# Batch 0's transposes on TensorE, the sign as a bit, and two token groups in one pass over the weights

## The chip, the cores and the metric

The kernel runs on one core of a Trainium2 chip. The metric is the device time of one execution in microseconds (us). Its five engines (TensorE or PE, VectorE or DVE, ScalarE or ACT, GpSimd or POOL, SyncE or SP) each work through their own queue in order, and the 16 DMA engines move data beside them. The time before is the median of three runs.

## The reference

Causal attention with a decay, then a SwiGLU block, then a mixture of eight experts of which each token uses one:

```python
q, k, v: (4, 8, 576, 64)   f: (4, 8, 576)          # batch, head, position, dim
cum    = cumsum(log(clip(f, 1e-4, 1)))
scores = q @ k.T / 8 + cum[:, None] - cum[None, :]   # causal
x      = softmax(scores) @ v                          # -> (2304, 512)
h      = silu(x @ w_gate) * (x @ w_val)               # (512, 1536), float64 weights
y      = h @ w_out                                    # (1536, 512), float64
e      = argmax(y @ r_gate); p = softmax(y @ r_gate)[e]
out    = p * (relu(y @ w1[e]) @ w2[e])                # 8 experts, 512 x 1024 x 512
```

## The kernel before

**Three stages.** Attention goes over 16 pairs of heads, four pairs (`NP`) to a batch. A pair has four items: two heads, each with the first three blocks of queries (g=0) and the last two (g=1). `slot(i)` runs `part1` (scores, maximum, exponential) of item i, `part2` (the split of the probabilities into a high and a low 16-bit half, and their transposition) of item i-1, and `pv` (probabilities times v) of item i-2. The SwiGLU block goes over nine groups of 256 tokens, in six units each (j, 256 of the 1536 inner columns): `unit_g` and `unit_v` make 24 TensorE products each into the banks `g` and `v`, a Tanh on ScalarE (L526), two VectorE steps (L529, L536), a split, and `unit_o` one unit later adds 12 products (L556) to the two banks `y0` and `y1`; `fin0` copies these out when a group is complete. The experts are the third stage.

**Weights.** The three SwiGLU weights arrive as float64. `decode` makes a float32 tile of 128 x 512 from a fetch of 512 KB, looked at as pairs of 32-bit words `lo` and `hi`: ScalarE takes the absolute value of `hi` as a float (L878) and its sign (L879), VectorE shifts by three bits (L880) and joins the top bits of `lo` (L881), GpSimd multiplies by the sign (L884). There are 36 of these. `w_dec`, `w_split` and `wo_dec` are the tasks round them; `mark[j]` and `markw[j]` say which tasks unit j needs. Fetches land in `wgb`, `wvb` while those are free, and in the one buffer `raw`.

**Transposition by DMA.** `prep` scales q and k of a head, splits them into halves (L230, L234, L235) and has a DMA transpose them from `qks` to `qkt` (L237). `score` adds two products, (qh, kh) and (qh, kl side by side with ql), and a decay term and mask. `part2` casts a row of probabilities to 16 bits (L349, VectorE), subtracts for the low half (L352, L363, GpSimd) and has a DMA transpose the lot into `pt` (L366), which `pv` reads (L387). After the second head, `xn` is normalised (L400) and for batch 0 transposed by TensorE (L429) into `xr`, the input of the units, by L440 (ScalarE) and L441 (VectorE).

**Order.** Python code emits the slots, tasks and units in a fixed sequence, and a scheduler with a timeline of its own sets each engine's queue from it. First 18 slots (`first`, batch 0) with 43 tasks among them; then units 0 to 53, each preceded by the tasks it needs (`mark[u]`, six units) and by slots that `pace` hands out along the points `pts_`: none until unit 4, batch 1 until unit 10, and so on.

```python
pts_ = [(-1, first), (NJ - 2, first), (2 * NJ - 2, 8 * NP + 2), (4 * NJ - 1, 12 * NP + 2), (6 * NJ - 2, NSL)]
```

PSUM has eight banks: three for scores, one for `px`, and one each for `g`, `v`, `y0`, `y1`.

Of the kernel before, what the change touches and what calls it, by code (L numbers as in the profile page):

```python
# [27 lines left out]
def kernel(  # L28
# [37 lines left out]
    g_d = dram.tile([NT + 1, 1], F32, name="g_d")  # L66
# [19 lines left out]
    cnt = const.tile([128, NE], F32, name="cnt")  # L86
    sv = const.tile([128, 2, B], F32, name="sv")
# [9 lines left out]
    def consts():  # L97
# [32 lines left out]
        vec.memset(cnt, 0.0)  # L130

# [24 lines left out]
    qk_in = [ap_.tile([128, 2, NCH, D], F32, name=f"qk_in{i}") for i in range(NQK)]  # L156
# [16 lines left out]
    def load_heads(t, src, b, h):  # L173
        sp.dma_start(out=t[64:128, :, 0, :], in_=src[b, h:h + 2, 0:64, :].rearrange("h p d -> p h d"))
        for hh in range(2):
            sp.dma_start(
                out=t[:, hh, 1:NCH, :], in_=src[b, h + hh, 64:S, :].rearrange("(c p) d -> p c d", p=128)
            )

    def load_qk(P, a):  # L180
        if P < NPAIR:
            load_heads(qk_in[(2 * P + a) % NQK], (q, k)[a], P // NP, 2 * (P % NP))
# [32 lines left out]

    def prep(P, hh):
        sc, c = stt[P]
# [20 lines left out]
        heads[P, hh] = (qkt, c[1][:, hh, :])  # L238
# [129 lines left out]

    pxs = {}

    def pv(i):
# [9 lines left out]
        for m in range(nt):  # L381
            last = base + m
            pm, o = pt[m]
# [136 lines left out]

    def unit_g(u):
        g, j = divmod(u, KF // 2)
# [9 lines left out]
    def unit_v(u, t):  # L532
        g, j = divmod(u, KF // 2)
# [12 lines left out]
    def unit_o(u):  # L546
        g, j = divmod(u, KF // 2)
        hi, lo = hbuf.pop(u)
        if j == 0:
            yps[g] = [ps_y.tile([128, DM], F32, tag=f"y{i}", name="yp") for i in range(2)]  # L550
        for i in range(2):
            n_ = 0
            for fi in range(2):
                fk = 2 * j + fi
                for hx, wx in ((hi, 0), (hi, 1), (lo, 0)):
# [4 lines left out]
                        start=(j == 0 and n_ == 0),  # L560
                        stop=(j == KF // 2 - 1 and n_ == 5),
# [76 lines left out]
    def fin2(g):  # L638
# [96 lines left out]
        rows_out(g_d, g, gw)  # L735
# [37 lines left out]
    def start():  # L773
# [25 lines left out]
        act.dma_start(out=g_d[NT:NT + 1, :], in_=zr[:, 0:1])  # L799
# [71 lines left out]
    def decode(src, n):  # L871
        c = c_tile()
        raw = fetch(src, n, c.rearrange("p (a n) -> p a n", a=n))
        if raw is not None:
# [3 lines left out]
            act.activation(out=c, in_=hi.bitcast(F32), func=ACTF.Abs, scale=2.0 ** -112)  # L878
            act.activation(out=hi.bitcast(F32), in_=hi, func=ACTF.Sign)  # L879
# [4 lines left out]
            gp.tensor_tensor(out=c, in0=c, in1=hi.bitcast(F32), op=ALU.mult)  # L884
# [37 lines left out]
    NJ = KF // 2  # L922
# [179 lines left out]
    def unit(u, between=None):  # L1102
# [5 lines left out]
        if u > 0:  # L1108
            if u - 1 < NJ:
                upto(markw[u - 1])  # L1110
            unit_o(u - 1)
            g1, j1 = divmod(u - 1, NJ)
# [10 lines left out]
            if j1 == NJ - 1:  # L1123
                if g1 == 0:
# [23 lines left out]
    PRE0, PRE = 2, 43  # L1148
# [16 lines left out]
    pts_ = [(-1, first), (NJ - 2, first), (2 * NJ - 2, 8 * NP + 2), (4 * NJ - 1, 12 * NP + 2), (6 * NJ - 2, NSL)]  # L1165
# [7 lines left out]
    for u in range(NU + 1):  # L1173
        if u < NJ:
            upto(mark[u])
        if u < NU and u % NJ == 0:
            for b, _, _ in spans(min(u // NJ + 1, NG - 1)):
# [4 lines left out]
        if u < NU:  # L1182
            need = 4 * NP * ((G * (u // NJ + 1) - 1) // S + 1) + 2
        tgt = pace(u)
        slots(need)
        unit(u, lambda: slots(min(tgt, nslot[0] + 1)))
# [162 lines left out]

    def gate(s, t):  # L1350
# [129 lines left out]
```

## Time and profile before

| what | us |
|---|---|
| runs, median of 3 (lowest to highest) | 1014.65 (1012.99 to 1016.63) |
| the profiled execution | 1012.41 |
| its span | 1010.6 |
| busy: PE / DVE / ACT / POOL | 882.2 / 614.9 / 555.3 / 389.6 |

The profiled execution is one run with the hardware profiler; its time and its span, from the first instruction to the last, differ by 1.8 us. Rows of a timeline have start and duration in us; consecutive instructions overlap a little. In lists by line, the two numbers after the count are busy us in all and mean ns of one. An arrow in a wait list points at what released the wait. PEclk is the granted clock of TensorE as a share of 2.4 GHz.

### The profile page before, as it was taken

To read this page: it belongs to the slowest core of one execution; us is meant where nothing else is said; L and a number is where in the kernel's file an instruction comes from. 1 tells how busy PE (TensorE), PEld (TensorE's weight loads), DVE (VectorE), ACT (ScalarE), POOL (GpSimd) and SP (SyncE) were. 2 spreads that over 40 slices of the span, in tenths; PEclk is the share of its full clock that TensorE was granted. 3 is DMA by queue.
4 is the path that set the end of the run, shared out by engine and by line. 5 is a ranking of instruction groups with operands and counts; after the bars stand their busy time and mean duration, and the time that the engine had idled before them with its cause. 6 is when DMAs were issued, how large, how long until landed. Compare 5 with 4: busy or idle time off the path is not lost.

```text
span 1010.6 us, 19838 instructions
## 1 busy us (share of the span) xinstructions
PE 882.2 (87%) x7028; PEld 734.7 (73%) x7053; DVE 614.9 (61%) x1818; ACT 555.3 (55%) x1205; POOL 389.6 (39%) x467
## 2 busy tenths in 40 slices
PE   1545557998999989999999999898989999999995
PEld 0334336877777868888878888687869788889894
DVE  6999888487666746565644434334536675665540
ACT  5987988476677666665633322122425454555431
POOL 1468676464444425344442222222245632100101
PEclk9995657999999999999999999899989999999998
DMA  8897998347886787567545422112376887765420
GB/s 244 209 216 205 230 204 187 90 101 165 180 172 146 164 190 158 101 133 137 102 113 143 121 22 64 5 18 66 71 180 187 218 219 201 215 198 159 132 95 34
DMA packets 309481, 146.35 MB, mean 145 GB/s; under 512 B 273441, under 2 KB 285857, under 8 KB 309380
## 3 DMA queue, kind: packets, MB, share of 16 engines
q1 hardware_dynamic: 305088, 134.68, 56.2%
q0 software_dynamic: 4096, 10.24, 3.7%
q8 instruction: 56, 0.92, 0.4%
q14 instruction: 45, 0.37, 0.2%
q10 hardware_dynamic: 196, 0.14, 0.0%
HBM read 84.24 MB, written 10.31 MB: 94 GB/s over the span
## 4 chain that ended last, share of the span: by engine, by line
PE 46%; DMA 17%; issue 12%; DVE 6%; ACT 3%; SPq 2%; POOL 2%; POOLq 0%; DVEq 0%; ACTq 0%
PE yp L556 11%; PE g L503 10%; PE v L503 10%; DMA out_dram<-o,ix 5%; PE bank L1218 3%; DMA pt<-p 3%; PE px L387 2%; DMA pair<-yt 2%; PE bank L1261 2%; DMA pair<-words 2%; DMA wr<-in_moe_w_dram 1%; PE ps L262 1%; PE ps L263 1%; DVE wlo L978 1%; PE ps L265 1%
## 5 line engine op out<-in xcount | busy, mean ns | idle before, releaser
L352 POOL TENSOR_TENSOR p<-st,p 128x128 f16<-128x128 f32 (+3 forms) x128 | 110.1, 864 | 102.1 <-issue 62.7
L543 POOL TENSOR_TENSOR lo<-t,hi 128x512 fp32r<-128x512 f32 x54 | 70.1, 1299 | 149.3 <-ACT hi L542 121.6
L503 PE MATMUL g<-xr,wga 128*128 128x256 f16 x864 | 106.1, 277 | 0.3 <-DVE t L529 0.3
L503 PE MATMUL v<-xr,wva 128*128 128x256 f16 x864 | 106.2, 277 | 0.0
L327 ACT ACTIVATE st<-st,nb,c 128x64 f32<-128x64 f32 (+4 forms) x160 | 102.6, 643 | 0.9
L503 PEld LDWEIGHTS <-wga 128*128 128x128 f16 x864 | 82.6, 100 | 17.2 <-issue 6.6
L503 PEld LDWEIGHTS <-wva 128*128 128x128 f16 x864 | 84.8, 101 | 10.6 <-issue 0.3
L387 PE MATMUL px<-vs,pt 128*128 128x64 f16 x1280 | 56.3, 203 | 39.3 <-DMA pt<-p 28.8
L349 DVE CAST p<-st 128x64 f16<-128x64 f32 (+4 forms) x160 | 68.4, 442 | 31.6 <-ACT st L327 20.1
L317 DVE CUSTOM_DVE_ANT_0 st<-ps,zero 128x64 f32<-128x64 f32 (+3 forms) x160 | 55.8, 377 | 50.9 <-PE ps L270 48.8
L387 PEld LDWEIGHTS <-pt 128*128 128x128 f16 x1280 | 50.3, 105 | 49.3 <-DMA pt<-p 32.8
L363 POOL TENSOR_TENSOR p<-st,p 128x64 f16<-128x64 f32 (+1 forms) x128 | 54.1, 424 | 70.6 <-issue 36.4
L262 PE MATMUL ps<-qkt 128*128 128x64 f16 (+2 forms) x192 | 56.5, 312 | 21.1 <-DMA qkt<-qks 7.2
L526 ACT ACTIVATE t<-g,gscale 128x512 f32<-128x512 f32 (+3 forms) x72 | 39.4, 573 | 62.2 <-PE g L503 59.0
L1012 POOL DMA_INDIRECT out_dram<-o,ix x24 | 24.6, 1026 | 123.3 <-ACT o L1263 79.5
L542 ACT ACTIVATE hi<-t 128x512 fp32r<-128x512 f32 x54 | 33.8, 625 | 56.5 <-DVE t L536 56.5
L556 PE MATMUL yp<-wohi,hi 128*128 128x512 f32 x144 | 60.6, 421 | 0.0
L263 PE MATMUL ps<-qkt 128*128 128x64 f16 (+2 forms) x192 | 60.1, 315 | 0.0
L1223 ACT ACTIVATE h<-bank 128x320 fp32r<-128x320 f32 (+1 forms) x64 | 26.3, 422 | 60.1 <-PE bank L1218 59.8
L1225 DVE SCALAR_TENSOR_TENSOR h<-bank,h 128x64 fp32r<-128x64 f32 (+2 forms) x128 | 33.4, 305 | 40.4 <-ACT h L1223 40.4
L556 PE MATMUL yp<-wohi,lo 128*128 128x512 f32 x144 | 57.6, 402 | 0.0
L556 PE MATMUL yp<-wolo,hi 128*128 128x512 f32 x144 | 57.1, 397 | 0.0
(322 smaller groups left out, 2483.2 us busy)
## 6 DMA issues: line engine op xcount, KB each, us to landing
wr<-in_moe_w_dram SPq DMA_DIRECT2D x72, 512.0 KB, 5.1
vr<-in_v_dram SPq DMA_DIRECT2D x16, 288.0 KB, 4.5
qk_in<-in_q_dram SPq DMA_DIRECT2D x32, 128.0 KB, 2.5
qk_in<-in_k_dram SPq DMA_DIRECT2D x32, 128.0 KB, 2.6
v_in<-in_v_dram SPq DMA_DIRECT2D x32, 128.0 KB, 3.0
y_d<-ys SPq DMA_DIRECT2D x6, 512.0 KB, 3.5
wgb<-in_moe_w_gate_dram SPq DMA_DIRECT2D x5, 512.0 KB, 5.9
raw<-in_moe_w_val_dram SPq DMA_DIRECT2D x5, 512.0 KB, 4.2
```

The source lines that it names most:

```text
L262: pe.matmul(out=ps[:, o:o + n], lhsT=lq, rhs=qkt[:, 1, k0:k1], start=True, stop=False, skip_group_check=True)
L263: pe.matmul(out=ps[:, o:o + n], lhsT=lq, rhs=qkt[:, 2, k0:k1], start=False, stop=False, skip_group_check=True)
L317: vec.tensor_tensor_reduce(out=sts[m][:, k0 - 64:k1 - 64], in0=ps[:, o:o + n], in1=zero.to_broadcast([128, n]), scale=1.0, scalar=init, op ...
L327: act.activation(out=sts[m], in_=sts[m], func=ACTF.Exp, scale=c[:, 0:1], bias=nb[:, m:m + 1], accum_out=sm[:, m, hh:hh + 1],)
L349: vec.tensor_copy(out=flat[:, o + 64:o + 64 + n], in_=src)
L352: gp.tensor_tensor(out=flat[:, o1:o1 + n - 64], in0=src[:, 64:n], in1=flat[:, o + 128:o + 64 + n], op=ALU.subtract)
L363: gp.tensor_tensor(out=blk[:, :, 0:64], in0=pair, in1=blk[:, :, 64:128], op=ALU.subtract)
L387: pe.matmul(out=px[:, 128 * m + 64 * hh:128 * m + 64 * hh + 64], lhsT=pm[:, o + ph * last + c, :], rhs=vs[:, hh, c, vh, :], start=(c == 0 ...
L503: pe.matmul(out=ps[:, fi, :], lhsT=w16[:, kk, wi, 128 * fi:128 * fi + 128], rhs=xr[:, kk, x0:x0 + 2, xi, :], start=(n_ == 0), stop=(n_ == ...
L526: act.activation(out=t[:, :, c0:c1], in_=gps[:, :, c0:c1], func=ACTF.Tanh, scale=gscale[:, b, j:j + 1])
L543: last["lo"] = gp.tensor_tensor(out=lo, in0=t, in1=hi.bitcast(F32), op=ALU.subtract)
L556: pe.matmul(out=yps[g][i], lhsT=hx[:, fi, 128 * i:128 * i + 128], rhs=wo[fk][wx], start=(j == 0 and n_ == 0), stop=(j == KF // 2 - 1 and n ...
```

## The change

**Order of units.** Units no longer run group by group at the start: `order` is group 0's units 0 to 2, all six of group 1, group 0's units 3 to 5, and then the rest as before. So weights of unit j are used by two groups in one sweep. Group 0's sums of the first three units are copied from `y0`, `y1` to DRAM by `part_out` and read back in `fin0(0)`, which adds them to the sums of the last three. 27 tasks instead of 43 stand among the first 18 slots; the others come during units 0 to 4, and those from the 19th on are fetched no earlier than q of batch 1's first pair. `pts_` loses the point that held batch 1 back until unit 4.

**Sign as a bit.** `decode` copies `hi` with its sign (Copy in place of Abs), drops the Sign and the multiplication, and lets VectorE join the sign bit of `hi` (L1003).

**Batch 0 without DMA transposes.** `prep0` transposes q and k of a pair as float32 on TensorE (L250), two heads at once, and ScalarE and VectorE split them from PSUM (L256, L257, L263, L264); the heads are kept apart by masks in the scale `qm`, which makes three products of a score where two were. `turn_p` transposes the float32 probabilities on TensorE (L449, 4 blocks a bank, banks `g`, `v`, `y0`, `y1` in turn), ScalarE copies the high half (L453) and VectorE subtracts for the low one (L454). Batches 1 to 3 keep the DMA transposes.

**Gate weights.** They were written to DRAM and gathered for the overflow tile; now `gate_of` computes them anew from that tile's x.

```diff
+    ring4 = [(ps_g, "g"), (ps_g, "v"), (ps_y, "y0"), (ps_y, "y1")]
...
+    def prep0(P):
+        sc, c = stt[P]
+        qm = st_p.tile([128, 2], F32, tag="qm", bufs=2, name="qm")
+        vec.tensor_scalar(out=qm, in0=half, scalar1=sc[:, 0, 0:1], scalar2=None, op0=ALU.mult)
...
+            for x in range(NCH):
+                o = ps[:, 128 * x:128 * x + 128] if x < NCH - 1 else last_[:, 128 * a:128 * a + 128]
+                pe.transpose(out=o, in_=src[:, :, x, :], identity=ident)
...
+                        act.activation(out=two[h][:, 0, n0:n1], in_=p, func=ACTF.Copy, scale=qm[:, h:h + 1])
+                        vec.scalar_tensor_tensor(
+                            out=two[h][:, 1, n0:n1], in0=p, scalar=qm[:, h:h + 1], in1=two[h][:, 0, n0:n1],
+                            op0=ALU.mult, op1=ALU.subtract,
+                        )
...
+            heads[P, h] = ([(qh, kh), (ql, kh), (qh, kl)], c[1][:, h, :])
...
+    def turn_p(i):
...
+        for blks in BLKS[g]:
+            ps = quad()
+            for x, (m, c) in enumerate(blks):
+                src = st[:, 0:128] if m == 0 else sts[m - base][:, max(128 * c - 64, 0):max(128 * c + 64, 128)]
+                pe.transpose(out=ps[:, 128 * x:128 * x + 128], in_=src, identity=ident)
...
+            act.activation(out=h_, in_=ps[:, 0:128 * w], func=ACTF.Copy)
+            vec.tensor_tensor(out=l_, in0=ps[:, 0:128 * w], in1=h_, op=ALU.subtract)
...
+    CUT = 3
+    order = (
+        [(0, j) for j in range(CUT)] + [(1, j) for j in range(NJ)] + [(0, j) for j in range(CUT, NJ)]
+        + [(g, j) for g in range(2, NG) for j in range(NJ)]
+    )
...
+    def part_out():
+        r = [c_p.tile([128, DM], F32, tag="c", name="yc") for _ in range(2)]
+        act.activation(out=r[0], in_=yps[0][0], func=ACTF.Copy)
+        vec.tensor_copy(out=r[1], in_=yps[0][1])
+        for i in range(2):
+            sp.dma_start(out=y_d[r0_of(i):r0_of(i) + 128, :], in_=r[i])
...
+        if g == 0:
+            rows_out(y_d, g, ys, True)
+            for i in range(2):
+                vec.tensor_tensor(out=ys[:, i, :], in0=ys[:, i, :], in1=yps[g][i], op=ALU.add)
...
-            act.activation(out=c, in_=hi.bitcast(F32), func=ACTF.Abs, scale=2.0 ** -112)
-            act.activation(out=hi.bitcast(F32), in_=hi, func=ACTF.Sign)
+            act.activation(out=c, in_=hi.bitcast(F32), func=ACTF.Copy, scale=2.0 ** -112)
...
-            gp.tensor_tensor(out=c, in0=c, in1=hi.bitcast(F32), op=ALU.mult)
+            vec.scalar_tensor_tensor(
+                out=ci, in0=hi, scalar=-2 ** 31, in1=ci, op0=ALU.bitwise_and, op1=ALU.bitwise_or
+            )
...
+            if done[0] < 18:
+                tasks[done[0]]()
+            else:
+                with tc.issue_after(qload[4, 1].ins):
+                    tasks[done[0]]()
...
-    PRE0, PRE = 2, 43
+    PRE0, PRE = 2, 27
...
-    pts_ = [(-1, first), (NJ - 2, first), (2 * NJ - 2, 8 * NP + 2), (4 * NJ - 1, 12 * NP + 2), (6 * NJ - 2, NSL)]
+    pts_ = [(-1, first), (2 * NJ - 2, 8 * NP + 2), (4 * NJ - 1, 12 * NP + 2), (6 * NJ - 2, NSL)]
...
+        if u < 2 * NJ:
+            upto(27 + (len(tasks) - 27) * (u + 1) // 5)
...
+    def gate_of(xt, ps, pool, dst):
+        p = ps("t")[:, 0:NE]
+        prods = [(x, kk) for kk in range(KD) for x in xt]
+        for n_, (x, kk) in enumerate(prods):
+            pe.matmul(
+                out=p, lhsT=x[:, kk, 0:128].bitcast(F32), rhs=rg[:, kk, 0:NE], start=(n_ == 0),
+                stop=(n_ == len(prods) - 1), skip_group_check=True,
+            )
```

VectorE's queue, in batch 0's slots, where weights are decoded between the items. Before:

```order
L880 TENSOR_SCALAR wo<-wo 128x512
L349 CAST p_1_108<-st 128x64
L349 CAST p_1_108<-st 128x192
L349 CAST p_1_108<-st 128x320
L881 SCALAR_TENSOR_TENSOR wo<-wvb,wo 128x512
L880 TENSOR_SCALAR wo<-wo 128x512
L881 SCALAR_TENSOR_TENSOR wo<-wgb,wo 128x512
L349 CAST p_2_109<-st 128x448
L349 CAST p_3_110<-st 128x576
L880 TENSOR_SCALAR wo<-wo 128x512
```

The place that answers to it after the change (L999 and L1000 are the shift and the join that were L880 and L881):

```order
L1003 SCALAR_TENSOR_TENSOR wo<-wgb,wo 128x512
L454 TENSOR_TENSOR p_1_108<-g,pt 128x512
L1003 SCALAR_TENSOR_TENSOR wo<-wvb,wo 128x512
L257 SCALAR_TENSOR_TENSOR qk_506<-ps,qm,qk_506 128x128
L1000 SCALAR_TENSOR_TENSOR wo<-raw,wo 128x512
L999 TENSOR_SCALAR wo<-wo 128x512
L935 TENSOR_SCALAR sw<-tot 128x1
L938 COPY sw<-tot 128x1
L454 TENSOR_TENSOR p_2_109<-v,pt 128x512
L454 TENSOR_TENSOR p_2_109<-yp,pt 128x128
```

The casts of the probabilities are gone from the row, and sign joins (L1003) and subtractions from PSUM (L454, L257) stand between the decoding steps.

SyncE's queue in the same part. Before:

```order
L861 DMA wvb<-in_moe_w_val_dram 128x4x256
L366 DMA_TRANSPOSE pt<-p_0_107 128x9x128
L174 DMA v_in_106<-in_v_dram 64x2x64
L176 DMA v_in_106<-in_v_dram 128x4x64 x2
L187 DMA v_in_106<-in_v_dram 64x2x64
L237 DMA_TRANSPOSE qkt<-qks 128x15x128
L366 DMA_TRANSPOSE pt<-p_1_108 128x9x128
L237 DMA_TRANSPOSE qkt<-qks 128x15x128
L366 DMA_TRANSPOSE pt<-p_2_109 128x7x128
L366 DMA_TRANSPOSE pt<-p_3_110 128x9x128
```

After (L981 is the weight fetch, L179, L181 and L195 are the loads of q, k and v):

```order
L981 DMA wvb<-in_moe_w_val_dram 128x4x256
L179 DMA qk_in_103<-in_q_dram 64x2x64
L981 DMA raw<-in_moe_w_out_dram 128x1024
L179 DMA qk_in_105<-in_k_dram 64x2x64
L181 DMA v_in_106<-in_v_dram 128x4x64
L179 DMA v_in_106<-in_v_dram 64x2x64
L181 DMA v_in_106<-in_v_dram 128x4x64
L195 DMA v_in_106<-in_v_dram 64x2x64
L981 DMA wgb<-in_moe_w_out_dram 128x1024
L181 DMA qk_in_105<-in_k_dram 128x4x64 x2
```

The transposes that stood among the loads are gone here; only fetches and loads follow one another.

TensorE's queue between two items of batch 0. Before:

```order
L387 LDWEIGHTS pt
L387 MATMUL px<-vs,pt 128x64
L429 MATMUL px<-ident,xn 128x128 x3
L805 MATMUL tot<-am,onesf 128x2
L805 MATMUL tot<-totw,onesf 128x1
L262 LDWEIGHTS qkt
L262 MATMUL ps<-qkt 128x64
L263 LDWEIGHTS qkt
L263 MATMUL ps<-qkt 128x64
```

After (L527 is the transposition of `xn`, L322 the products of the scores):

```order
L250 MATMUL ps<-ident,qk_in_104 128x128
L527 MATMUL px<-ident,xn 128x128 x3
L449 MATMUL yp<-ident,st 128x128 x5
L449 MATMUL g<-ident,st 128x128 x4
L449 MATMUL v<-ident,st 128x128
L322 LDWEIGHTS qk_1309
L322 MATMUL ps<-qk_1308,qk_1309 128x64
L322 LDWEIGHTS qk_1309
L322 MATMUL ps<-qk_1308,qk_1309 128x64
L322 LDWEIGHTS qk_1309
L322 MATMUL ps<-qk_1309 128x64
```

The item's scores now follow ten transposes of probabilities (`st`) into three banks, and a score has three products.

## Rows read from the trace of the kernel before

**Rows 1.** The page's slices: TensorE, tenths of 25 us each.

```profile
PE   1545557998999989999999999898989999999995
```

**Rows 2.** Table by stretch: stretch, length, then busy us of each engine, PEclk, DMA share, GB/s.

```profile
0.00:25.00 25.00, 2.93 (x10) 2.50 (x10) 15.80 (x55) 14.88 (x33) 4.46 (x15) 1.00 0.86 244
10.00:166.00 156.00, 79.88 (x649) 57.43 (x655) 136.11 (x381) 136.38 (x335) 93.75 (x102) 0.74 0.91 223
0.00:224.00 224.00, 136.17 (x1131) 104.73 (x1139) 184.66 (x513) 178.78 (x424) 128.73 (x148) 0.82 0.77 189
224.00:395.00 171.00, 160.12 (x1628) 129.49 (x1635) 113.62 (x378) 117.77 (x312) 78.49 (x116) 0.98 0.77 166
```

**Rows 3.** Timeline of VectorE: first steps of units 0 and 6 (start, us, instruction).

```profile
166.40 0.68 DVE L529 SCALAR_TENSOR_TENSOR t<-t,g 128x512 f32<-128x512 f32 x1
...
223.67 0.67 DVE L529 SCALAR_TENSOR_TENSOR t<-t,g 128x512 f32<-128x512 f32 x1
```

**Rows 4.** What TensorE waited for, 0 to 250 us: us in total, times, longest.

```profile
PE px L387 <- DMA pt<-p: 21.0, 9, 4.7
...
PE px L429 <- DVE xn L400: 10.0, 5, 4.3
...
PE ps L262 <- DMA qkt<-qks: 5.7, 2, 3.9
PE ps L262 <- DVE mx L317: 5.6, 4, 2.1
```

**Rows 5.** What VectorE waited for, 10 to 166 us.

```profile
DVE c L880 <- ACT c L878: 5.6, 3, 3.9
```

**Rows 6.** Timeline: L881 beside a busy GpSimd, and with GpSimd idle.

```profile
141.09 1.47 POOL L884 TENSOR_TENSOR wo<-wo,wgb 128x512 f32<-128x512 f32 x1
...
141.45 1.66 DVE L881 SCALAR_TENSOR_TENSOR c<-raw,c 128x512 int32<-128x512 int32 x1
...
217.27 0.69 DVE L881 SCALAR_TENSOR_TENSOR c<-raw,c 128x512 int32<-128x512 int32 x1
```

**Rows 7.** VectorE by line and shape, 0 to 166 us.

```profile
L349 DVE CAST p<-st 128x576 f16<-128x576 f32 x8 | 8.0, 996 | 0.0
...
L317 DVE CUSTOM_DVE_ANT_0 st<-ps,zero,mx 128x512 f32<-128x512 f32 x8 | 6.0, 744 | 0.2
L881 DVE SCALAR_TENSOR_TENSOR wo<-wvb,wo 128x512 int32<-128x512 int32 x6 | 5.9, 982 | 0.0
...
L441 DVE TENSOR_TENSOR xr<-px,xr 128x256 f16<-128x256 f32 x7 | 2.9, 408 | 0.0
```

**Rows 8.** VectorE and ScalarE by line and shape, 166 to 221 us.

```profile
L526 ACT ACTIVATE t<-g,gscale 128x512 f32<-128x512 f32 x7 | 4.7, 671 | 0.0
...
L529 DVE SCALAR_TENSOR_TENSOR t<-t,g 128x512 f32<-128x512 f32 x6 | 4.1, 681 | 5.1 <-ACT t L526 5.1
```

**Rows 9.** ScalarE and GpSimd by line and shape, 0 to 166 us.

```profile
L879 ACT ACTIVATE wgb<-wgb 128x512 f32<-128x512 int32 x12 | 7.9, 655 | 0.0
...
L884 POOL TENSOR_TENSOR wo<-wo,wgb 128x512 f32<-128x512 f32 x7 | 10.3, 1471 | 1.9 <-ACT nb L323 1.9
```

**Rows 10.** Timeline of TensorE: fp32 transposes and g products, early and late.

```profile
58.77 0.90 PE L429 MATMUL px<-ident,xn 128*128 128x128 f32 x3 [4.31 <-DVE xn L400]
...
161.59 2.11 PE L503 MATMUL g<-xr,wga 128*128 128x256 f16 x9
...
554.95 1.03 PE L627 MATMUL ps<-ident,ys 128*128 128x128 f32 x8
```

**Rows 11.** The chain that ended last: a fetch at 135 us, g at 176 us.

```profile
135.51 4.32 DMA raw<-in_moe_w_gate_dram
...
176.65 2.63 PE g L503 x24
```

**Rows 12.** DMA issues, 0 to 166 us: count, median us to landing.

```profile
pt<-p SPq DMA_TRANSPOSE x24, 3.2
...
qkt<-qks SPq DMA_TRANSPOSE x10, 4.6
```

More of the change, by code (lines that the diff above doesn't have):

```diff
@@ L86 @@
     cnt = const.tile([128, NE], F32, name="cnt")
+    half = const.tile([128, 2], F32, name="half")
     sv = const.tile([128, 2, B], F32, name="sv")
@@ L155 @@
     NQK, NV, NPB, NBLK = 3, 1, 4, 9
-    qk_in = [ap_.tile([128, 2, NCH, D], F32, name=f"qk_in{i}") for i in range(NQK)]
+    qk_in = [
+        ap_.tile([128, NCH, 2, D], F32, name=f"qk_in{i}").rearrange("p c h d -> p h c d") for i in range(NQK)
+    ]
     v_in = [ap_.tile([128, 2, NCH, D], F32, name=f"v_in{i}") for i in range(NV)]
@@ L338, in p16_of @@
         return p16s[n % NPB].rearrange("p a t -> p (a t)"), 128 * OFF[m] if g == 0 else 0
+    BLKS = (
+        [[(0, 0), (2, 0), (2, 1), (2, 2)], [(1, 0), (1, 1)]],
+        [[(3, c) for c in range(4)], [(4, c) for c in range(4)], [(4, 4)]],
+    )
     def part2(i):
         P, (hh, g) = i // 4, items[i % 4]
+        if P < NP:
+            turn_p(i)
+            return
         sts = pend.pop(i)
@@ L382, in pv @@
             last = base + m
+            if P < NP:
+                prods = [(c, vh, ph) for c in range(last + 1) for vh, ph in ((0, 0), (1, 0), (0, 1))]
+                for n_, (c, vh, ph) in enumerate(prods):
+                    r = slice(0, 128 if c else 64)
+                    pe.matmul(
+                        out=px[:, 128 * m + 64 * hh:128 * m + 64 * hh + 64], lhsT=pt[0][ph][r, pt[1][last, c], :],
+                        rhs=vs[r, hh, c, vh, :], start=(n_ == 0), stop=(n_ == len(prods) - 1), skip_group_check=True,
+                    )
+                continue
             pm, o = pt[m]
@@ L532, in unit_v @@
     def unit_v(u, t):
-        g, j = divmod(u, KF // 2)
+        g, j = order[u]
         vps = gv(g, j, 1, "v")
@@ L1108, in unit @@
         if u > 0:
-            if u - 1 < NJ:
-                upto(markw[u - 1])
+            g1, j1 = order[u - 1]
+            if g1 < 2:
+                upto(markw[j1])
             unit_o(u - 1)
-            g1, j1 = divmod(u - 1, NJ)
+            if (g1, j1) == (0, CUT - 1):
+                part_out()
             if g1 == NG - 1 and j1 < len(EP["w2"]):
@@ L1173 @@
     for u in range(NU + 1):
[L1174 to L1177, printed above, removed]
+        g, j = order[min(u, NU - 1)]
+        if u < 2 * NJ:
+            upto(mark[j])
+        if u < NU and (u == 2 * NJ - 1 or u % NJ == 0 and u >= 2 * NJ):
+            for b, _, _ in spans(min((u + 1) // NJ + (u % NJ == 0), NG - 1)):
                 if b not in unscaled:
@@ L1393 @@
                 turn(xts[nxt % 2], xgs[nxt])
+                if nxt == NE:
+                    gate_of(xts[nxt % 2], bank, ix_p, gwo)
         if nxt == NE:
```

117 lines of the change are left out of this document (86 added, 31 removed).

## The prediction

> **What bounds the kernel now.** Read the page's slices first [rows 1]. TensorE is nearly full from the eighth slice on (a slice is 25 us), and thin in the first seven. The table by stretch puts numbers on it [rows 2]: from 10 to 166 us TensorE is busy for 80 of 156 us at a granted clock of 0.74, VectorE for 136, ScalarE for 136, and DMA holds 0.91. Unit 0's first VectorE step starts at 166.4, that of unit 6 at 223.7 [rows 3]. From there TensorE is the bound: up to 395 it works 160 of 171 us. So time comes from two places: how early the units get going, and how much TensorE work still lies behind that moment.
>
> In the first stretch the wait lists matter [rows 4]. TensorE waits 21.0 us for transposed probabilities (`pt`) and 5.7 us for transposed q and k, both DMA results; VectorE's longest wait in the stretch is 5.6 us for ScalarE's L878 [rows 5], and the chain of waits shows a `raw` weight fetch ahead of it that took 4.3 us [rows 11]. VectorE is busy 184.7 of the first 224 us, so DMA waits can give back little unless VectorE gets shorter: I treat VectorE as the bound up to that step of unit 6 (the seventh in order, in either kernel), and TensorE as the bound behind it.
>
> **The change, part by part.** Counts are from the instruction orders of the two kernels, up to unit 6's first VectorE step. In the timeline a VectorE step starts some 0.08 us before its predecessor's row ends, so I charge a row's time less 0.08.
>
> *New on VectorE.* 36 sign joins (L1003), two SBUF inputs of 512 columns like L881, which took 0.69 us with GpSimd idle [rows 6]: 36 x 0.61 = 22 us. 24 subtractions (L454) and 12 split steps of 512 columns from PSUM, priced as L529, 0.681 [rows 8]: 36 x 0.60 = 21.6. 16 narrower subtractions and 12 narrow splits as L441's 256 columns, 0.408 [rows 7]: 28 x 0.33 = 9.2. Sum +53.
>
> *Gone from VectorE.* 25 probability casts (L349, 320 columns in the mean; 576 take 0.996 us beside GpSimd [rows 7], by L881's ratio of 0.69 to 1.66 [rows 6] 0.41 without, so about 0.24 in the mean): -6 uncontended. Eight splits of q and k (L234), by estimate half a us each: -4.
>
> *Moved ahead.* `pace` no longer holds batch 1's slots back until unit 4, so four more second-half and two more first-half score items of batch 1 run before unit 6: 5,248 columns at L317's 0.744 per 512 [rows 7] = 7.6, plus four splits of v, six normalisations and single steps, by estimate half a us each, in all 13 us, on TensorE another 13 (below). With one copy for `part_out`, VectorE's uncontended work up to unit 6 goes up by 53 - 10 + 13.5 = 56 us.
>
> *GpSimd.* L884 (36 multiplications, 1.47 us a piece [rows 9]) and batch 0's L352 and L363 go. GpSimd's work up to unit 6 falls from 129 us [rows 2] to 58. VectorE pays for GpSimd: the same L881 took 1.66 us while L884 ran on GpSimd and 0.69 when GpSimd was idle [rows 6]. Pricing all VectorE instructions up to unit 6 by their rows with an idle GpSimd gives 139 us, by their rows as they ran 176: 37 us for 129 us of GpSimd, 0.3 each. So 58 us will cost 17, and 20 us come back. Net for VectorE: 56 - 20 = +36, so 221 instead of 185 us busy.
>
> A sentence from the Trainium skill belongs beside this: GPSIMD Engine Reference, section "Key points", says that GpSimd shares its SBUF interfaces with VectorE and contends with instructions in a 2-port mode or with two SBUF inputs. The L881 rows agree. By that rule L1003 is exposed and L454, with PSUM as one input, is not; if all 36 joins ran at the 0.98 us that L881 shows for `wvb` [rows 7] instead of 0.61, the sum would be 13 us worse.
>
> *The transposes.* 32 DMA transposes of batch 0 go: 24 of 3.2 us and 8 of 4.6 us from issue to landing [rows 12], which is what TensorE's 21.0 and 5.7 us waited for. Instead TensorE makes 160 fp32 transposes. Eight L627 in the later part took 1.03 us, three L429 in this stage 0.90 [rows 10]; with the last one's own 0.27 and 0.42 off, that is 0.11 and 0.24 from start to start: 18 to 38 us. A third score product adds 12,800 columns: 24 g products of 256 columns take 2.63 us on the full clock [rows 11], 0.11 each, and nine at 161 us take 2.11 [rows 10], 0.21 each, so 5 to 10. With 40 more pv products, 24 to 50 us of TensorE in all, before unit 0, where it is idle for 76. I charge nothing for it, because VectorE's work is longer; rivals 2 and 3 are what happens if that cover fails.
>
> *ScalarE.* 36 L879 of 0.655 [rows 9] go, -20 after overlap. 40 copies and 24 splits from PSUM come; as L526, 0.671 for 512 columns [rows 8], they are 36 x 0.58 + 28 x 0.3 = +29. With the moved slots, about 10, ScalarE is busy for 179 + 19 = 198 us up to unit 6, below VectorE's 221. Off the path.
>
> *The shared pass.* Sharing takes little out of the time before unit 0: the order has 29 decodes ahead of it before, 27 now, and 36 either way by unit 6. It lets decoding overlap units that have work, nothing else. It costs a write of y to DRAM, a read back and two additions in `fin0(0)` of 0.6 us each. The `y0`, `y1` banks wait for those and for `part_out`'s copies, hidden while the next unit's g and v run (2.63 us each [rows 11]); if L697 queues behind 6 us of VectorE work, it costs 1 to 3 us. `issue_after` holds the last decodes until batch 1's first loads: SP only, already behind them.
>
> *gate_of.* Eight fp32 products and a short chain in the expert part, where TensorE is the bound: +1.5, between 0 and 3.
>
> *The sum.* Unit 6's step: 221 busy, the 9 us that VectorE idles in the first 25 [rows 2], and 5 of waits: from there to 166 it idled 12 (20 from 10 us on, 8 of them before 25), of which over half goes back to fetches and transposes; what it idled behind 166 it spent waiting for TensorE. That is 235, 11 later than now. Behind it TensorE has 13 us less to do: a head's scores are 1,600 columns times three products, at 0.11 us per 256 that is 2.1 us, plus masks, pv and transposes about 3.5, times almost four heads. And of the 11 us that TensorE idles between 224 and 395, 4 go by estimate, as batch 1 no longer presses. Then +1.5. Result: 11 - 13 - 4 + 1.5 = -4.5. The profiled execution took 1012.4 us, 2.2 below the median of the runs, which is 1014.65, inside their spread; -4.5 gives 1008 from the one and 1010 from the other. I forecast **1008 us**.
>
> **Rivals.**
>
> 1. *Faster, 993.* VectorE loses even the rest of its contention (-10: what remains on GpSimd runs beside PSUM steps) and its last waits (-5): unit 6's step comes at 220, and -4.5 becomes -19.5. For it: half of VectorE's new work reads PSUM, and L317's mean from PSUM, 0.744 in a stretch full of GpSimd work [rows 7], shows nothing like L881's step to 1.66. Against: VectorE waits for results of a chain now, not only for data.
>
> 2. *Slower, 1027: the chain through PSUM.* In batch 0 every one of 16 items now goes TensorE, ScalarE (hi), VectorE (lo), TensorE, through four banks in a fixed turn, each engine in order. L454 sits in VectorE's queue behind joins and shifts of decodes that wait for fetches; what is queued behind a waiting L454 is the next L317, for which ScalarE's exponentials and TensorE's next scores wait. A pattern of this kind is in the trace: TensorE's fp32 L429 waits 10.0 us, five times, up to 4.3, for VectorE's L400 [rows 4]. At 1.2 us an item this is 16 x 1.2 = 19, so -4.5 becomes +14.5. It decides from 0.3 us an item, where the 4.5 us are eaten. For it: four decodes' steps in a row stand between L454s in the order. Against: two slots lie between an item's scores and its pv.
>
> 3. *Slower, 1019: TensorE at its lower level bounds batch 0.* From 10 to 166 us the granted clock is 0.74 [rows 2], and by the nine products at 161 us much of that is spent at 1.2 GHz. In the first 25 us TensorE works 2.9 [rows 2]; 25 + 80 + 50, and 16 of the kind that it waits for VectorE now (10.0 for L400, 5.6 for L317 [rows 4]), put unit 0's step at 171. VectorE, with 138.5 us of uncontended work and 7 for GpSimd ahead of that step, and the 9 and 5 us of idle, would allow 160: 11 us late, +6.5. The Trainium skill, VectorE: DVE Perf Modes, section "The three transpose paths", gives 390 ns for a TensorE transpose of 128x128 (bf16) against 1309 for a DMA one: by it the 160 would be an estimated 62 us and TensorE full. The L627 and L429 rows, 0.11 and 0.24 a piece, speak for less.
>
> 4. *No change, 1013: the pass does not do what its name says.* 27 decodes stand before unit 0 instead of 29, VectorE is as long as it was, and what unit 6 loses is what TensorE gains.
>
> **How the numbers follow.** Forecast (1004 to 1011) 0.36; rival 1 0.16; rival 4 (1011 to 1018) 0.18; rival 2 0.21; rival 3 0.09. A measurement of this kernel tells about 0.3%, 3 us, from no change, so faster means below 1011.6: 0.36 + 0.16 = 0.52; same 0.18; slower 0.21 + 0.09 = 0.30. The range leaves out half of rival 2 and a third of rival 1, some 0.16: 990 to 1027, which holds the 13 us of the contended joins as well.
>
> **What would show it.** Right: no `pt` row in TensorE's waits before unit 0; VectorE busy near 221 us at unit 6's step, and that step at 230 to 240; TensorE's work between units 6 and 20 smaller by about 13; L1003 near 0.7. Wrong: VectorE or TensorE rows that wait for ScalarE's L453 or for a `g`, `v` or `yp` bank by more than 6 us in batch 0 (rival 2); TensorE over 130 us busy before unit 0 at the same granted clock (rival 3); unit 6's step before 224 (rival 1); or a TensorE idle stretch among units 3 to 8, waiting for batch 1's `pt`, whose transposes stand on SP behind fetches into the one `raw` buffer.

## The result, and the profile after

The changed kernel takes **987.1 us** (median; 986.1 to 989.6) beside 1015.6 for the kernel before (median of four, one more than in the table above): a ratio of 0.972, 95% interval 0.969 to 0.976. That is some 28 us faster. The forecast was 1008, in a range from 990; the direction was right, the 7 us that it gave were a quarter of what came, and the range missed the result by 3 us.

The page's slices of the changed kernel, TensorE alone, answer to [rows 1]:

```profile
PE   3688669879999999999999999999999999999995
```

The batch-0 stretch is still thin, but less so, and there are no dips behind it: the kernel before has five 8s behind its eighth slice, three of them between 632 and 758 us (the last of these in the expert part), and this one has only 9s there. So part of the gain lies far behind the place where the code was changed most. The table by stretch, of the changed kernel, answers to [rows 2] (columns as there):

```profile
10.00:166.00 156.00, 111.11 (x989) 81.63 (x990) 145.67 (x452) 143.80 (x376) 23.86 (x25) 0.87 0.65 171
0.00:235.00 235.00, 174.71 (x1592) 132.18 (x1592) 213.46 (x644) 197.81 (x499) 56.59 (x74) 0.90 0.70 169
231.00:298.00 67.00, 64.65 (x649) 53.83 (x647) 43.40 (x136) 43.48 (x108) 31.96 (x42) 1.00 0.84 158
298.00:382.00 84.00, 83.03 (x826) 69.69 (x825) 52.23 (x171) 53.45 (x139) 35.21 (x49) 1.00 0.75 140
```

and the first VectorE steps of units 0 and 6 to [rows 3]:

```profile
159.40 0.67 DVE L634 SCALAR_TENSOR_TENSOR t<-t,g 128x512 f32<-128x512 f32 x1
...
234.72 0.69 DVE L634 SCALAR_TENSOR_TENSOR t<-t,g 128x512 f32<-128x512 f32 x1 [0.17 <-ACT t L631]
```

Unit 0's step comes 7 us earlier, unit 6's 11 us *later* (223.7 before). From there on TensorE works 148 of 151 us. To find the 28 us, I cut the execution at the ends of units' g products on TensorE (numbered in order of execution) and take the time of each piece (profiled executions, which lie 25.8 us apart):

| piece, us | before | after | difference | forecast |
|---|---|---|---|---|
| start to unit 6 | 219.3 | 231.5 | +12.2 | +11 |
| unit 6 to 20 | 175.3 | 150.7 | -24.6 | -17 |
| unit 20 to 53 | 329.0 | 318.1 | -10.9 | 0 |
| unit 53 to the end (experts) | 287.0 | 284.5 | -2.5 | +1.5 |
| span | 1010.6 | 984.8 | -25.8 | -4.5 |

Three things ask for a cause: the third row, of which the forecast says nothing, the second, which it has too small, and how the first two hang together.

### The profile page after: what moved, and what is told of

It reads as the page before. It is cut to its first block, busy times and chain, and to the rows that moved or that the text cites. A ratio compares the mean times of both kernels' runs of the same rounds, so it can differ in the third digit from the quotient of the medians.

```text
span 984.8 us, 20192 instructions
## 1 busy us (share of the span) xinstructions
PE 901.6 (92%) x7317; PEld 751.1 (76%) x7317; DVE 624.5 (63%) x1876; ACT 551.1 (56%) x1210; POOL 302.6 (31%) x366
## 4 chain that ended last, share of the span: by engine, by line
PE 42%; DMA 9%; issue 7%; DVE 3%; ACT 1%; POOL 1%; SPq 0%; POOLq 0%; DVEq 0%; ACTq 0%
PE yp L663 10%; PE v L601 9%; PE g L601 9%; PE bank L1347 4%; PE bank L1390 3%; DMA pair<-words 3%; DMA out_dram<-o,ix 3%; PE ps L322 1%; DMA pt<-p 1%; PE px L485 1%; DMA xg<-y_d,ix 1%; DVE wlo L1102 1%; DMA xr<-xs 1%; DVE wolo L1102 1%; PE ps L327 1%
## 5 line engine op out<-in xcount | busy, mean ns | idle before, releaser
L422 POOL TENSOR_TENSOR p<-st,p 128x128 f16<-128x128 f32 (+1 forms) x96 | 82.0, 857 | 115.2 <-issue 65.2
L601 PE MATMUL v<-xr,wva 128*128 128x256 f16 x864 | 103.1, 273 | 0.6 <-DVE p L454 0.6
L419 DVE CAST p<-st 128x448 f16<-128x448 f32 (+3 forms) x120 | 48.7, 412 | 34.6 <-ACT st L389 32.8
L433 POOL TENSOR_TENSOR p<-st,p 128x64 f16<-128x64 f32 x96 | 43.0, 448 | 79.4 <-issue 34.9
L322 PE MATMUL ps<-qkt 128*128 128x64 f16 (+4 forms) x288 | 53.7, 288 | 7.8 <-DVE mx L379 4.7
L1352 ACT ACTIVATE h<-bank 128x320 fp32r<-128x320 f32 (+1 forms) x64 | 26.1, 422 | 57.8 <-PE bank L1347 57.5
L327 PE MATMUL ps<-cum,nc 128*128 128x64 bf16 (+2 forms) x192 | 55.2, 294 | 0.0
L385 ACT ACTIVATE nb<-mx,addc,c 128x3 f32<-128x3 f32 (+1 forms) x64 | 24.7, 386 | 52.4 <-DVE mx L379 51.9
L641 DVE SCALAR_TENSOR_TENSOR t<-t,hscale,v 128x512 f32<-128x512 f32 (+3 forms) x72 | 42.4, 609 | 16.1 <-PE v L601 15.7
```

The source lines that it names most:

```text
L322: pe.matmul(out=ps[:, o:o + n], lhsT=lq[:, 128 * j:128 * j + 128], rhs=rk_[:, k0:k1], start=(x == 0), stop=False, skip_group_check=True,)
L327: pe.matmul(out=ps[:, o:o + n], lhsT=pk, rhs=cum3[:, k0 - 64:k1 - 64], start=False, stop=(k1 <= d0), skip_group_check=True,)
L419: vec.tensor_copy(out=flat[:, o + 64:o + 64 + n], in_=src)
L422: gp.tensor_tensor(out=flat[:, o1:o1 + n - 64], in0=src[:, 64:n], in1=flat[:, o + 128:o + 64 + n], op=ALU.subtract)
L433: gp.tensor_tensor(out=blk[:, :, 0:64], in0=pair, in1=blk[:, :, 64:128], op=ALU.subtract)
L601: pe.matmul(out=ps[:, fi, :], lhsT=w16[:, kk, wi, 128 * fi:128 * fi + 128], rhs=xr[:, kk, x0:x0 + 2, xi, :], start=(n_ == 0), stop=(n_ == ...
```

## The third piece: the writes of the gate weights

Between units 20 and 53 the two kernels do the same SwiGLU work. What differs is that before, each group's routing wrote 256 gate weights of 4 bytes to DRAM (`rows_out(g_d, g, gw)`). The changed kernel computes eight columns for one tile instead. The DMA issues of the kernel before from 540 to 724 us (count, KB each, median us to landing) show what such a write takes:

```profile
y_d<-ys SPq DMA_DIRECT2D x2, 512.0 KB, 3.3
...
ys<-y_d SPq DMA_DIRECT2D x3, 256.0 KB, 6.6
...
g_d<-gw SPq DMA_DIRECT2D x5, 1.0 KB, 8.7
g_d<-gw SPq DMA_DIRECT2D x4, 0.2 KB, 6.8
```

One KB takes 8.7 us, a quarter of it still 6.8. On SyncE's queue transpositions of y (`pair`, L620) stand right behind some of these writes (issues on that queue, start and us):

```profile
624.69 1.74 SPq L571 DMA_DIRECT2D g_d<-gw  x3
626.55 1.28 SPq L620 DMA_TRANSPOSE pair<-yt  x1
...
683.47 1.32 SPq L620 DMA_TRANSPOSE pair<-yt  x1
687.51 0.82 SPq L571 DMA_DIRECT2D g_d<-gw  x2
689.30 1.24 SPq L620 DMA_TRANSPOSE pair<-yt  x1
```

These three transpositions are in the chain that ended last of the kernel before, here from issue to landing:

```profile
626.55 9.21 DMA pair<-yt
...
683.47 4.88 DMA pair<-yt
...
689.30 6.31 DMA pair<-yt
```

The two that were issued within 2 us behind writes took 9.2 and 6.3 us, the one at 683.47, with no write just ahead of it, 4.9. Behind the first and the last TensorE stands still for `rk` (4.7 us at 637, 2.6 at 698). Its operand `rb` does not come from that transposition, since TensorE makes no product between the two: VectorE's copy out of `pair` (L623) waits for it, and the last routing steps of an earlier group, up to `rb` (L736), stand behind that copy in VectorE's queue (timeline; in brackets the idle time before a step and what ended it):

```profile
635.85 0.45 DVE L623 COPY yt<-pair 128x512 uint16<-128x512 uint16 x1 [6.86 <-DMA pair<-yt]
...
636.98 0.20 DVE L736 TENSOR_TENSOR rb<-eq,gw 128x48 f32<-128x48 f32 x1
...
637.23 1.09 PE L716 MATMUL rk<-rb,ra 128*128 128x48 f32 x4 [4.72 <-DVE rb L736]
```

TensorE's wait list from 395 to 724 us has one large row:

```profile
PE rk L716 <- DVE rb L736: 7.3, 2, 4.7
```

In the changed kernel no such row is left, and its chain has no `pair` piece from unit 20 to 53.

**Put back in the changed kernel** (the writes alone; nothing reads them):

```diff
+    g_d = dram.tile([NT + 1, 1], F32, name="g_d")
...
         vec.reciprocal(out=gw, in_=ge)
+        rows_out(g_d, g, gw)
```

> The changed kernel with one thing put back: each group's gate weights are written to DRAM again (256 values of 4 bytes a group, on SyncE's queue); nothing reads them. Theory Q (these writes hold up the transposes of y behind them in the groups 6 to 8, and that was worth some 11 us of the gain, which the prediction did not price): about 998 us, 995 to 1001, and a transposition of y of 7 to 9 us near unit 45. Rival A (the wait there came from how the slots and units fell, which the new order changed): 985 to 990, no long transposition.

Measured: 1001.7 us, ratio 0.989 (0.983 to 0.995), some 15 us more than the changed kernel and 0.7 above theory Q's range. Its chain has the pieces back, and TensorE's wait list from 381 to 710 us the row:

```profile
613.00 9.08 DMA pair<-yt
...
669.84 4.70 DMA pair<-yt
...
675.48 6.27 DMA pair<-yt
```

```profile
PE rk L839 <- DVE rb L859: 7.0, 2, 4.6
```

Units 44 to 45 take 16.8 us with the writes and 9.1 without, units 50 to 53 30.3 and 26.1: 11.9 us, the same 16.9 and 30.5 as in the kernel before.

**Taken from the kernel before** (writes gone, `gate_of` in place of the gather):

```diff
-        rows_out(g_d, g, gw)
...
+                if nxt == NE:
+                    gate_of(xts[nxt % 2], bank, ix_p, gwo)
```

> The kernel before with one thing taken away: the writes of the gate weights to DRAM; the overflow tile's gate weights are computed anew, as in the changed kernel. Theory Q: 1015 - 11 = about 1004 us (1000 to 1007). Rival A: 1012 to 1017, the long waits near units 45 and 51 stay.

Measured: 1003.6 us, ratio 0.990 (0.985 to 0.995), 10 us less, and units 44 to 45 take 9.1 us. The `rk` row is gone from TensorE's waits, and the last group's two transpositions in the chain read:

```profile
677.18 4.91 DMA pair<-yt
683.04 3.06 DMA pair<-yt
```

The one that took 6.3 us behind a write takes 3.1 without; the other is as it was. From unit 20 to 53 the changed kernel with the writes takes 329.0 us, as the kernel before, and the kernel before without them 317.5, as the changed one (318.1): the writes are the whole of the third row. Theory Q holds from both sides, and rival A falls.

**Issued elsewhere.** Is it SyncE's queue, which stands until the weights are ready, or the transfer?

```diff
-        rows_out(g_d, g, gw)
+        rows_out(g_d, g, gw, eng=act)
```

> The kernel before with the same writes of the gate weights issued from ScalarE's queue and not from SyncE's. If what costs is that SyncE's queue stands still until the gate weights are ready (order of issue), the gain is as in the run without them, about 1004 us. If what costs is the transfer itself (256 descriptors of 4 bytes take 6 to 9 us in the DMA engines, and a transposition that starts meanwhile shares them), it stays near 1012 to 1017, with transpositions of y of 8 to 9 us.

Measured: 1022.3 us, ratio 1.007 (1.004 to 1.009), slower than before, and above both alternatives. Its chain has three long `pair` pieces within units 38 to 53 and not two, and TensorE waits three times (540 to 735 us):

```profile
573.68 9.05 DMA pair<-yt
...
634.54 8.03 DMA pair<-yt
...
697.21 7.13 DMA pair<-yt
```

```profile
PE rk L716 <- DVE rb L736: 12.0, 3, 4.7
```

So the place in SyncE's queue is not what costs most. A transposition issued up to 2 us behind such a write, or (at 573.68) 0.2 us ahead of one, takes 6.3 to 9.2 us in these runs, whichever engine issued the write. Nor is it special to transpositions: the reads `ys<-y_d` of 256 KB, 6.6 us in the kernel before, take 2.5 in the changed one (530 to 702 us):

```profile
ys<-y_d SPq DMA_DIRECT2D x3, 256.0 KB, 2.5
```

What in the transfer takes the time, no run here tells. The Trainium skill (DMA: Bandwidth & Descriptors, section "Specifications") says that transfers below 512 B are done as a read, a change and a write; that would fit, but no run here shows it. The section gives no price; set against the 4-byte rows of `g_d` it could have pointed at this term, and not sized it.

## The first two pieces: what lets batch 1 run early

**The point in `pace` put back in the changed kernel**, so that batch 1's slots wait for unit 4 again:

```diff
-    pts_ = [(-1, first), (2 * NJ - 2, 8 * NP + 2),
+    pts_ = [(-1, first), (NJ - 2, first), (2 * NJ - 2, 8 * NP + 2),
```

> The changed kernel with the point put back that holds batch 1's slots until unit 4. Theory M (TensorE work of batch 1 moved ahead of unit 6 into time that VectorE bounds, 13 us forecast): unit 6 comes some 8 us earlier, the units behind it lose 13, so 990 to 994 us. Rival: the slots find room among TensorE's idle time either way, 985 to 989.

Measured: 1005.8 us, ratio 0.990 (0.984 to 0.995): 18 us slower, four times what was expected. Unit 6 is there 20 us earlier, at 211.8, and unit 20 20 us later, at 402.3. (The profiled execution, 1010.8 us, was the slowest of its four, so the second 20 is an upper figure.) The table by stretch of this version, units 6 to 12 and 12 to 20, and TensorE's waits in the first of them:

```profile
212.00:312.00 100.00, 84.27 (x858) 66.79 (x863) 69.84 (x232) 69.72 (x185) 47.53 (x72) 0.97 0.89 162
312.00:402.00 90.00, 83.99 (x819) 68.98 (x822) 50.64 (x169) 54.76 (x141) 35.09 (x51) 0.94 0.76 148
```

```profile
PE px L485 <- DMA pt<-p: 9.3, 7, 3.1
PE ps L322 <- DMA qkt<-qks: 4.7, 4, 2.0
```

From unit 6 to 12 TensorE works 84 of 100 us where DMA holds 0.89: batch 1's splits and transposes are squeezed in there. Of its idle time, 14 us are waits for DMA.

**The same point taken out of the kernel before:**

```diff
-    pts_ = [(-1, first), (NJ - 2, first), (2 * NJ - 2, 8 * NP + 2),
+    pts_ = [(-1, first), (2 * NJ - 2, 8 * NP + 2),
```

> The kernel before with one thing changed: the point that holds batch 1's slots until unit 4 is gone. Theory M (what counts is that batch 1's chain of splits and DMA transposes gets units 0 to 5 to run in, instead of being squeezed between units 6 and 12, where the changed kernel with the point put back lost 18 us): unit 6 later by 8 us or so, unit 12 earlier than 308.8 by 8 or more, 1001 to 1008 us. Rival N (it pays only in the room on VectorE and DMA that the other edits make; alone batch 1's slots just delay units 0 to 5): 1011 to 1018.

Measured: 1018.7 us, ratio 1.004 (1.001 to 1.006): 4 us *slower*, just above rival N's range. Theory M falls in the form in which I had it; the units show why:

| end of unit's g, us | 0 | 6 | 12 | 20 | units 6 to 20 |
|---|---|---|---|---|---|
| before | 164.9 | 219.3 | 308.8 | 394.6 | 175.3 |
| before, without the point | 165.0 | 239.6 | 314.5 | 398.0 | 158.4 |
| changed, with the point | 156.5 | 211.8 | 312.1 | 402.3 | 190.5 |
| changed | 157.1 | 231.5 | 298.1 | 382.2 | 150.7 |

Taking the point out costs 20 us ahead of unit 6 in either kernel. Behind it the gain is 17 in the kernel before and 40 in the changed one. With the point in place, all that the other edits win ahead of unit 6 (219.3 to 211.8) is gone by unit 12: batch 1 sets the time, and an early unit 6 only waits longer. Without the point, but with the old batch 0, unit 6 is so late that the gain does not pay for it:

```profile
165.00:240.00 75.00, 64.49 (x646) 51.33 (x645) 57.21 (x159) 54.47 (x137) 42.25 (x53) 0.95 0.77 168
```

(the kernel before without the point, units 0 to 6: 64 of 75 us TensorE, 57 VectorE). Neither is worth anything alone: with the point the changed kernel is 8 us ahead of the kernel before, of which the gate weights' writes are 10 or more; without it and with the old batch 0 it is 4 behind. Together they are worth, by difference, about 16 of the 28 us. Why units 6 to 20 take 190 us in the third row and 175 in the first, both with the point, I have not settled; part of it may be that slow execution. The DMA share in units 6 to 12 is 0.89 in the one, and 0.74 in the other, by the table of the kernel before over units 6 to 12 and 12 to 20:

```profile
219.00:309.00 90.00, 82.52 (x850) 65.40 (x851) 64.48 (x216) 64.58 (x172) 44.74 (x68) 0.98 0.74 159
309.00:395.00 86.00, 82.61 (x832) 68.32 (x835) 54.14 (x180) 58.19 (x152) 38.75 (x56) 0.98 0.77 167
```

## Batch 0: which edits carry it

**Probabilities by DMA again**, q and k still by TensorE:

```diff
-        if P < NP:
-            turn_p(i)
-            return
...
-            if P < NP:
+            if P < 0:
                 prods = [(c, vh, ph) ...
```

> The changed kernel with the probabilities of batch 0 cast, split by GpSimd and transposed by DMA again; q and k are still transposed by TensorE. Forecast: VectorE is the bound before unit 0, the 40 subtractions cost it 20 us and the 40 casts 6 to 19, so unit 0 moves by less than 5 us: 984 to 992. Rival D (the DMA transposes and TensorE's waits for them, 21.0 us before, held batch 0, more than VectorE): unit 0 at 165 or later, 993 to 1002.

Measured: 991.3 us, ratio 0.976 (0.972 to 0.980), about 4 us slower by the medians, inside what the forecast allowed, with an interval that overlaps the changed kernel's (0.969 to 0.976).

**q and k by DMA again**, probabilities still by TensorE (`prep` without its branch to `prep0`):

> The changed kernel with q and k of batch 0 split first and transposed by DMA again (two products a score); the probabilities stay on TensorE. Undoing both cost 15 to 16 us, undoing the probabilities alone 4 to 6. If the two parts add up, this one costs about 10: 995 to 998 us. If either part alone frees most of what the DMA queue held (the rest of the waits is then hidden), each alone costs little and this one is at 988 to 992.

Measured: 988.6 us, ratio 0.976 (0.970 to 0.982), 2 to 3 us slower, inside the intervals: the second alternative.

**Both by DMA again:**

> The changed kernel with q, k and the probabilities of batch 0 all split and transposed by DMA again, as before the change. Forecast's theory (VectorE's work is the measure, and the new steps cost it 31 us while 16 splits, 40 casts and their GpSimd traffic go, some 40): 987 to 995 us. Rival D (TensorE's waits for DMA held batch 0, 26.7 us of them): 1000 to 1012, and those waits back in TensorE's list.

Measured: 1001.7 us, ratio 0.989 (0.985 to 0.994), 15 to 17 us slower, as rival D has it. By the medians the parts do not add up, 4 + 3 against 16. Each part alone is within the noise, so this rests on the traces as well: unit 20 ends 6, 1 and 14 us later than in the changed kernel. The first 157 us of the four versions, in the order changed, probabilities by DMA, q and k by DMA, both:

```profile
0.00:157.00 157.00, 105.08 (x919) 75.57 (x920) 144.24 (x463) 140.79 (x363) 19.21 (x30) 0.87 0.62 163
```

```profile
0.00:157.00 157.00, 96.83 (x837) 67.96 (x838) 141.67 (x439) 122.05 (x309) 63.47 (x94) 0.85 0.85 195
```

```profile
0.00:157.00 157.00, 97.97 (x802) 70.52 (x802) 137.25 (x444) 139.16 (x355) 17.67 (x29) 0.77 0.73 188
```

```profile
0.00:157.00 157.00, 80.32 (x723) 59.26 (x723) 128.71 (x403) 117.70 (x295) 65.34 (x92) 0.77 0.96 206
```

The DMA share is 0.62, 0.85, 0.73 and 0.96. With both, DMA is full, and TensorE's wait list has the row of [rows 4] back:

```profile
PE px L478 <- DMA pt<-p: 20.2, 8, 5.3
```

VectorE then works 129 of 157 us, 15 *less* than in the changed kernel, and the kernel is 16 us slower. GpSimd's work is back too, 65 of 157 us, but it is also back with the probabilities alone (63), which costs little. This speaks against the forecast's first reading, that VectorE bounds batch 0 and DMA waits can give back little: in the kernel before both were near full, VectorE at 136 of 156 us and DMA at 0.91. That DMA held the kernel before as much as it holds this version is inferred from here, not shown by a run of its own. (Unit 0's end is no mark here: in the versions with probabilities by DMA its products stand ahead of more of the attention in TensorE's order, behind 288 and 299 products into `px` and not 378, and are reached at 133 and 140 us. Unit 20 is the fair mark: 388.0 with the probabilities by DMA, 383.6 with q and k, 395.8 with both, 382.2 in the changed kernel.)

**The sign as before**, on ScalarE and GpSimd:

```diff
+            act.activation(out=hi.bitcast(F32), in_=hi, func=ACTF.Sign)
...
-            vec.scalar_tensor_tensor(
-                out=ci, in0=hi, scalar=-2 ** 31, in1=ci, op0=ALU.bitwise_and, op1=ALU.bitwise_or
-            )
+            gp.tensor_tensor(out=c, in0=c, in1=hi.bitcast(F32), op=ALU.mult)
```

> The changed kernel with the sign made as before: ScalarE's Sign and GpSimd's multiplication back, VectorE's 36 joins gone. By the forecast's sum VectorE gains 22 us and loses 36 x 1.4 x 0.3 = 15 to GpSimd's traffic, so 7 us less work on VectorE and 20 more on ScalarE (148 of the first 166 us busy): between -3 and +8, 985 to 996. Rival S (the decode chain over three engines and the wait for GpSimd is what held batch 0): unit 0 some 8 us later, 995 to 1003.

Measured: 994.1 us, ratio 0.978 (0.974 to 0.982), about 6 us slower (the intervals just overlap), near the upper end of what the forecast's sum allowed. The table of its first 157 us, beside that of the changed kernel above:

```profile
0.00:157.00 157.00, 106.18 (x885) 78.32 (x886) 130.62 (x410) 143.93 (x368) 46.02 (x51) 0.81 0.58 156
```

VectorE has 14 us less to do and ScalarE three more, at 144 of 157. So moving the joins to VectorE did not cost time and by the medians paid, although VectorE is the fuller engine. With the old sign unit 20 ends at 390.9, 9 us later, in a profiled execution (1000.0 us) that was the slowest of its four, 6 above their median. Whether it helps that the decode chain goes through one engine fewer (no GpSimd), or that ScalarE has less to do, is not shown.

**The units group by group**, no shared pass, no copy and no read back:

```diff
-    order = ([(0, j) for j in range(CUT)] + [(1, j) for j in range(NJ)] + ...
+    order = [(g, j) for g in range(NG) for j in range(NJ)]
...
-            if (g1, j1) == (0, CUT - 1):
-                part_out()
```

> The changed kernel with the units group by group again: no shared pass, no copy of half sums to DRAM, no read back; decoding and slots are handed out as in the changed kernel. Forecast's theory (the pass takes no decodes out of the time before unit 0 and is worth nothing by itself; part_out and the read back cost 1 to 3 us): 985 to 990 us. Rival P (without it group 0 alone needs all 36 decodes within six units, so units 1 to 5 wait for weights): 10 us and more behind, 996 to 1003, unit 6 no earlier than now.

Measured: 983.8 us, ratio 0.970 (0.967 to 0.973). That is at or below the changed kernel; both were measured again, side by side.

> The changed kernel itself, as the yardstick beside the version without the shared pass on the same chip: a ratio of 0.970 to 0.975 to the kernel before.

> The changed kernel without the shared pass, again, in more rounds. If part_out, the read back and the two additions cost what they took (1 to 3 us) and the pass gives nothing, its ratio to the kernel before is 0.001 to 0.003 below that of the changed kernel; if the pass is worth something, above it.

Measured: 985.2 us, ratio 0.973 (0.970 to 0.976), for the changed kernel, 986.6 and 0.973 (0.970 to 0.977) without the pass. No difference can be told: the shared pass, from which the change has part of its name, neither gives nor costs more than the 4 us or so that these intervals leave open. No version here beats the changed kernel beyond its interval.

## Why the forecast was wrong, by its own steps

**Up to unit 6: right, by two misses that cancel.** The step was forecast at 235 and came at 234.7. VectorE was busy for 213.5 us by then, not 221, and idle for 21.5, not 14. The parts miss as well, the other way round: the sum gave 13 us to batch 1's slots moved ahead, which leaves -2 of its 11 for all the rest; the versions with and without the point show 20 for the slots in either kernel, and -8 for the rest (219.3 to 211.8). That the step came out to 0.3 us is luck. The prices of single steps held: by line and shape up to 232 us, joins and subtractions of the changed kernel, and the shift's partner L1000, which was L881 in [rows 7],

```profile
L454 DVE TENSOR_TENSOR p<-g,pt 128x512 f16<-128x512 f32 x10 | 6.8, 677 | 0.0
...
L1003 DVE SCALAR_TENSOR_TENSOR wo<-wgb,wo 128x512 int32<-128x512 int32 x8 | 6.0, 746 | 0.0
...
L1000 DVE SCALAR_TENSOR_TENSOR wo<-wvb,wo 128x512 int32<-128x512 int32 x6 | 4.1, 679 | 0.0
```

took 0.68 to 0.75 us where the forecast's rows had 0.68 to 0.69. L1000 on `wvb` fell from 0.982 to 0.679 us, with GpSimd busy for 24 us between 10 and 166 in place of 94, so the relief is real (where a step still meets GpSimd it is as long as before: 1.75 us at 144.0 and 1.53 at 230.7); the Trainium skill's rule (GPSIMD Engine Reference, "Key points": shared SBUF interfaces) agrees with that, and the feared 13 us did not come. What VectorE waited for is in TensorE's list as well, from 0 to 250 us, and answers to [rows 4]:

```profile
PE yp L449 <- ACT st L389: 10.9, 6, 5.3
...
PE px L485 <- DMA pt<-p: 4.1, 3, 2.0
...
PE px L527 <- DVE xn L498: 2.5, 3, 1.1
PE v L449 <- DVE p L454: 2.4, 1, 2.4
...
PE g L449 <- DVE p L454: 1.6, 1, 1.6
```

DMA `pt` fell from 21.0 to 4.1 us, none of it before unit 0, as forecast, and 10.9 us for ScalarE's exponentials took its place. These feed the new transposes; they are not the wait for a bank that rival 2 named. For the banks TensorE waits 2.4 and 1.6 us, VectorE 1.9 us for L453, so no row reaches rival 2's 6 us: its chain exists, is short, and did not push unit 6 beyond the forecast. Rival 3 fell: TensorE was busy for 111 of 156 us at a granted clock of 0.87, not 130 at 0.74; six L449 at 60 us, 1.18 us with 0.34 for the last one, go by 0.17 each, inside the 0.11 to 0.24 that the rows gave.

**Units 6 to 20: the direction right, the size too small.** The step "13 us of TensorE work less, and 4 of its 11 idle" measured 17 and 8. TensorE's busy time fell from 165 us (219 to 395) to 148 (231 to 382); the granted clock rose from 0.98 to 1.00, and 2% of 165 is an estimated 3 us of that. Its idle time fell from 11 to 3. I had taken a third of the idle time "by estimate"; the version with the point put back, where TensorE waits 14 us for batch 1's transposes, shows what set it, and with the point gone little of that is left to wait for. The sum also counts this gain apart from the other edits; with the point alone taken out, the kernel before lost 4 us.

**Units 20 to 53: a term that was not there.** This is the step that failed: it takes the result out of the range. Under *gate_of* the forecast priced the eight products that came, and not the 14 small writes that went, so that units 20 to 53 stood in the sum at nothing. The wait list that it worked from stops at 250 us. The 7.3 us for `rk` and two `pair` transfers at 627 and 689 us stood in the trace of before, and [rows 1] had its dips there. The writes are worth 10 us (out of the kernel before) to 15 (into the changed one), 11 to 12 from unit 20 to 53. Of the 21 us between forecast and profiled span (-4.5 and -25.8) this term is 11, units 6 to 20 are 8, the experts 4, and the first piece takes 1 back; with this term in its sum the forecast would have been near 997, still 10 too slow, but its range would have held the result.

**The experts.** +1.5 was forecast, -2.5 came. In all the versions here this piece takes 282 to 291 us, with and without `gate_of`, so neither number is told apart from that spread.

**The shared pass** was forecast at next to nothing, with rival 4 asking whether nothing else would come either: the first holds within the 4 us above, the second does not.

**Rival 1** named a time, 993, near the result, but by an early unit 6 (under 224); that did not happen, so its mechanism is not what gave the 28 us.

## What to carry to other kernels

When an edit removes something small, price what it removes as carefully as what it adds, and far from the place of the edit: 14 transfers of at most 1 KB were worth 10 to 15 us, because transfers on the critical chain ran beside them. An edit that frees an engine early and an edit that moves work into the freed time may each be worth nothing alone, so a sum of single prices can miss the sign of either. And where two resources of a stage stand at nine tenths, the fuller one is not all there is to ask about: here VectorE was taken for the bound, and giving DMA its load back cost 15 to 17 us with VectorE working less. Ask of each what it would do if the other were free.

## What the runs showed of the hardware that was not expected

A write of 64 to 256 values of 4 bytes takes 6.8 to 8.7 us to land, against 3.3 for 512 KB of y in whole rows in the same stretch. A transposition of y issued beside it takes 6.3 to 9.2 us; the last one of these takes 3.1 when the writes are gone, and reads of y (256 KB) fall from 6.6 to 2.5. Issuing the write from another engine's queue does not mend that.
